# A fused retention and gated-sine MLP kernel: another order of steps for blocks 0 to 2, more casts on GpSimd, and batch 4's keys and values in runs of 64 tokens

## The chip, the core and the metric

The kernel runs on one core of a Trainium2 chip. The core has a tensor engine (PE in the profile), whose weight loads are shown apart (PEld), a vector engine (DVE), a scalar engine (ACT), GpSimd (POOL) and SyncE (SP), which here only issues DMAs. Each engine works through its own list of instructions in order and waits at an instruction until what it needs has been signalled. Sixteen DMA engines move data between HBM and the on-chip memory SBUF; the matmuls write to banks of a second memory, PSUM. The metric is the time of one execution on the device, in microseconds (us).

## The reference

The inputs are q, k and v with 8 batches, 8 heads, 576 tokens and a head size of 64, and the weights of an MLP: `w_in` (512 x 2048), `w_out` (2048 x 512) and `alpha` (2048).

```python
scores = (1 / sqrt(64)) * q @ k.T                 # per batch and head, 576 x 576
ret    = scores * Dmat                            # gamma_h ** (i - j) where i >= j, else 0
attn   = ret @ v                                  # no softmax
x = attn, heads side by side                      # 4608 x 512
h = x @ w_in                                      # 4608 x 2048
g = h + sin(alpha * h) ** 2 / (alpha + 1e-9)
out = g @ w_out                                   # 4608 x 512
```

All inputs and the output are 32-bit floats; on the chip the matmuls take 16-bit operands. Since the decay is a power of the distance between tokens, the kernel puts it into k and q as row factors and carries what lies behind a chunk of 128 tokens in a running state of k times v.

## The kernel before, in words

**Units of work.** The 4608 tokens are cut into nine blocks. Block n (0 to 7) holds the first 512 tokens of batch n; block 8 holds the last 64 tokens of all batches. For each block there are 16 projections (`project(n, fc)`, four matmuls of 128x512 each, L549), each followed by a sine on ACT (`sine`, L557), a square on ACT, VectorE or GpSimd (`square`, L566 or L568) and a product on VectorE (`product`, L573), which gives one sixteenth of g. The second gemm is cut into 16 steps too (`gemm2(n, u)`, L592, four matmuls of 128x512): u = 4c + part adds a quarter of the sum for the c-th 128 rows. After four parts `finish(n, c)` copies the rows out of PSUM and issues two output DMAs (L585).

**Attention of a batch.** It is done in two parts p of 256 tokens. `load(b, nm, p)` brings 512 KB of q, k or v (L148, or L143 for the form in runs of 64 tokens). `cast` turns them to 16 bits with the decay factors (L194 on DVE or POOL; values are copied, L119 or L121). q and k are then transposed: by TensorE (`turn`, L227) with a copy out of PSUM (`take`) in batches 0 and 1, by a DMA transpose on SyncE's queue (`crossed`, L217) from batch 2 on. `outer` makes k times v (L308), which `evict`, `take_sum`, `next_sum` (L337), `more` (L353, L354) and `to_state` (L344, L346) turn into running states. `scores` (L372) gives two heads' worth of products, `masked` (L384) applies the causal mask on VectorE, `values` (L414) and `add_states` (L436) give the attention's output in PSUM, and `keep` copies it to SBUF as x, the left operand of the projections.

**Token order.** Up to batch 4, partition i of a part holds tokens 2i and 2i+1, so one contiguous run of a load is 512 bytes long. From batch `HALVED` = 5 on, k and v are loaded with 64 neighbouring tokens on 64 partitions: a run is 256 bytes long and a load takes four DMAs of 128 KB, but half of the products of every second score group lie above the diagonal and are left out (64 of 128 columns), and so are a quarter of the masked columns.

**Order of the work.** For blocks 0 to 2 the order is a hand-placed list of calls under `tc.manual_schedule()`: the order of calls is the order on each engine, and the PSUM bank of each step is its last argument (h0, h1, h2, op, m0, m1). The table `BUFFERS` says which of the SBUF buffers each load, cast and so on takes in turn. From block 3 to block 8 a loop sets the order: projection u, its sine, attention of the next batch at some u, square, product, second gemm u of the block before. The list ends with batches 0 to 3 done and batch 4 loaded, cast and with its outer products made.

**DMA queues.** All loads of q, k, v, the DMA transposes and the outputs are issued by SyncE, in order; an issue waits until its buffer is free or its data are there, and all issues behind it wait too. `w_in` and `w_out` are loaded by GpSimd in four parts each (L109, L112), which turn them to 16 bits; w_out's rows lie so that each partition reads runs of 8 KB, in this kernel and in the changed one. `wait_for_w_out(g)` (L613) is a small DMA on SyncE that reads a loaded part of w_out, so SyncE stands until that part has landed. `fill_up` does the same `PAD` = 7 times in block 7.

**Fillers.** `keep_busy` (L605) lets TensorE multiply zeros while it has nothing to do at the start.

The changed functions and their callers, with the line numbers of the profile:

## Time and profile before

| | |
|---|---|
| median of 3 runs | 311.7 us (311.09 to 312.0) |
| the profiled execution | 309.53 us, of which its span 307.8 us |
| busy share of the span | PE 95%, DVE 64%, ACT 63%, POOL 42% |
| HBM | 36.75 MB read, 9.44 MB written, 150 GB/s over the span |

The page of the profile gives shares and the costliest groups: a group's line has the source line, engine, operation, the tiles written and read, the shape, the count, the busy time, the mean of one in ns, and the idle time before it with what ended it. A row of the timeline has start, duration, engine, line, operation and tiles. "x12" means twelve instructions merged into a row. A row of SPq is the time in which SyncE's sequencer issued a DMA, not the transfer itself. In the chain of waits a DMA's time runs from its issue to its landing. Matmul ends are modelled, so the distance between starts tells more than the duration of one.

### The profile page before, as it was taken

The numbers are of one execution on the slowest core, as the hardware profiler recorded it, in microseconds if no ns is written. First come the engines' busy times: TensorE is split into PE (matmuls) and PEld (weight loads), VectorE is DVE, ScalarE is ACT, GpSimd is POOL, SyncE is SP. The second block draws the span as 40 slices with busy tenths as digits, with TensorE's granted clock in tenths as the row PEclk, the third lists the DMA queues.
The fourth block names the chain that finished last, engine by engine and source line by source line (L and its number), as shares of the span: only waits on it lengthen the run. The fifth ranks groups of instructions, "written<-read, shape, count | busy, mean of one in ns | idle before, by whom it ended". The sixth has DMA issues, their size and how long they took to land.

```text
span 307.8 us, 7895 instructions
## 1 busy us (share of the span) xinstructions
PE 291.3 (95%) x3225; PEld 156.3 (51%) x3225; DVE 197.2 (64%) x281; ACT 193.3 (63%) x323; POOL 128.9 (42%) x149
## 2 busy tenths in 40 slices
PE   3879999999799999999999999799999999999995
PEld 1758555555355654554455445444455454444443
DVE  2867796968576876867665686556656746655600
ACT  3748877994278668665776577556774456555411
POOL 2767774467664556686159626833030000000000
PEclk9999999999999999999999999999999999999999
DMA  8999999999567398889799969966361121111132
GB/s 222 347 224 213 275 276 324 276 235 238 126 171 207 85 182 190 234 183 150 169 255 169 205 151 269 157 142 144 75 134 38 38 43 39 34 34 34 44 90 74
DMA packets 115620, 49.98 MB, mean 162 GB/s; under 512 B 71424, under 2 KB 110592, under 8 KB 115584
## 3 DMA queue, kind: packets, MB, share of 16 engines
q1 hardware_dynamic: 112064, 45.10, 63.1%
q0 software_dynamic: 2688, 4.19, 7.6%
q8 instruction: 25, 0.41, 0.6%
q10 hardware_dynamic: 832, 0.18, 0.4%
q14 instruction: 11, 0.09, 0.1%
HBM read 36.75 MB, written 9.44 MB: 150 GB/s over the span
## 4 chain that ended last, share of the span: by engine, by line
PE 82%; DMA 7%; issue 3%; POOL 2%; ACT 2%; DVE 2%; SPq 1%; POOLq 0%; DVEq 0%; ACTq 0%
PE ops L592 38%; PE hps L549 36%; PE o L414 2%; PE sc L372 2%; DMA raw<-in_k_dram 2%; DMA raw<-in_q_dram 2%; DMA raw<-in_v_dram 2%; PE kv L308 1%; ACT s L557 1%; DMA qT<-q 1%; POOL w_in L109 1%; SPq L148 1%; PE o L436 1%; DVE ret L384 1%; POOL k L194 1%
## 5 line engine op out<-in xcount | busy, mean ns | idle before, releaser
L592 PE MATMUL ops<-w_out,gT 128*128 128x512 f16 (+2 forms) x592 | 142.6, 374 | 0.1
L557 ACT ACTIVATE s<-hps,alpha_t 128x512 f16<-128x512 f32 x144 | 97.7, 685 | 69.4 <-PE hps L549 67.9
L573 DVE SCALAR_TENSOR_TENSOR gT<-ss,inva,hps 128x512 f16<-128x512 f16 x144 | 105.6, 745 | 52.5 <-ACT ss L566 47.9
L549 PE MATMUL hps<-xT,w_in 128*128 128x512 f16 (+1 forms) x544 | 126.9, 367 | 2.1 <-issue 2.0
L549 PEld LDWEIGHTS <-w_in 128*128 128x128 f16 x608 | 68.0, 114 | 58.2 <-issue 2.2
L592 PEld LDWEIGHTS <-gT 128*128 128x128 f16 x592 | 56.2, 98 | 63.0 <-issue 0.7
L568 DVE TENSOR_TENSOR ss<-s 128x512 f16<-128x512 f16 x62 | 34.9, 562 | 20.6 <-ACT s L557 20.0
L566 ACT ACTIVATE ss<-s 128x512 f16<-128x512 f16 x73 | 46.0, 631 | 1.4
L194 POOL TENSOR_TENSOR k<-raw,cn 128x1024 f16<-128x1024 f32 (+1 forms) x17 | 26.7, 1576 | 34.0 <-DMA raw<-in_k_dram 30.0
L119 ACT COPY osb<-ops 128x512 f32<-128x512 f32 (+1 forms) x33 | 19.2, 581 | 15.2 <-PE ops L592 13.8
L384 DVE TENSOR_TENSOR ret<-sc,mask 128x1024 f16<-128x1024 f32 x20 | 23.8, 1218 | 7.1 <-PE sc L372 7.1
L194 POOL TENSOR_TENSOR q<-raw,cn 128x1024 f16<-128x1024 f32 (+1 forms) x10 | 18.5, 1868 | 2.1 <-DMA raw<-in_q_dram 1.3
L353 POOL TENSOR_TENSOR s<-kvs,cn 128x256 f32<-128x256 f32 x21 | 13.7, 651 | 11.4 <-ACT kvs L119 11.3
L354 POOL TENSOR_TENSOR kvs<-s,kvs 128x256 f32<-128x256 f32 x21 | 16.0, 762 | 3.6 <-ACT kvs L119 2.2
L119 ACT CAST xT<-o 128x1024 f16<-128x1024 f32 (+1 forms) x13 | 12.6, 983 | 7.4 <-PE o L436 7.3
L121 POOL CAST v<-raw 128x1024 f16<-128x1024 f32 (+1 forms) x11 | 11.0, 998 | 14.6 <-DMA raw<-in_v_dram 14.6
L549 PE MATMUL hps<-xS,w_in 128*128 128x512 f16 x64 | 16.4, 379 | 0.0
L178 POOL TENSOR_TENSOR ks<-ks,cn 128x512 f16<-128x512 f32 x4 | 4.2, 1044 | 22.2 <-DMA vs<-in_v_dram 13.6
L568 POOL TENSOR_TENSOR ss<-s 128x512 f16<-128x512 f16 x9 | 9.3, 1038 | 8.9 <-ACT s L557 8.9
L414 PE MATMUL o<-ret,v 64*64 64x128 f16 (+1 forms) x512 | 11.6, 215 | 1.2 <-issue 0.7
L372 PE MATMUL sc<-qT,kT 64*64 64x128 f16 (+1 forms) x512 | 10.7, 215 | 1.8 <-DVE ret L384 1.0
L372 PEld LDWEIGHTS <-kT 64*64 64x64 f16 x512 | 7.6, 107 | 8.5 <-issue 6.7
(57 smaller groups left out, 153.7 us busy)
## 6 DMA issues: line engine op xcount, KB each, us to landing
out_dram<-osb SPq DMA_DIRECT2D x70, 128.0 KB, 2.5
raw<-in_q_dram SPq DMA_DIRECT2D x16, 512.0 KB, 5.9
raw<-in_k_dram SPq DMA_DIRECT2D x10, 512.0 KB
raw<-in_v_dram SPq DMA_DIRECT2D x10, 512.0 KB, 5.7
raw<-in_v_dram SPq DMA_DIRECT2D x24, 128.0 KB, 3.3
raw<-in_k_dram SPq DMA_DIRECT2D x24, 128.0 KB, 3.4
w_in<-in_moe_w_in_dram POOLq DMA_DIRECT2D x4, 512.0 KB, 11.3
w_out<-in_moe_w_out_dram POOLq DMA_DIRECT2D x4, 512.0 KB, 11.5
```

The lines of the kernel that those rows point to most:

```text
L119: eng.copy(d_, s_)
L194: eng.tensor_tensor(dst[:, a0:a1].rearrange("p a r t d -> p t (a r) d"), t_.rearrange("p (t a) x -> p t a x", t=2)[:, :, a0:a1].rearrange( ...
L354: nc.gpsimd.tensor_tensor(self.kvs[:, c], s32, self.kvs[:, c], ADD)
L372: matmul(sc[halves(g), t, c : c + n], kT[halves(t), 2 * a + r, halves(g)], qT[halves(t), 2 * a : 2 * a + 2, 64 * g + i0 : 64 * g + 64], st ...
L384: nc.vector.tensor_tensor(ret.rearrange("p t (z x) -> p (t z) x", z=2)[:, :, 0:n], sc.rearrange("p t (z x) -> p (t z) x", z=2)[:, :, 0:n], ...
L414: made.append(matmul(o[t][halves(e), c : c + 128].rearrange("p (r i) -> p r i", r=2)[:, :, i0:64], v16[halves(g), 4 * t + 2 * x + e, r, :] ...
L549: matmul(hps_of[n, fc][0][:, cols], w_in16[fc // 4][:, a, fc % 4 :: 4], xs[n][:, a, cols], start=(a == 0 and part != 1), stop=(a == KT - 1 ...
L557: nc.scalar.activation(s_t, hps, mybir.ActivationFunctionType.Sin, bias=0.0, scale=alpha_t[:, fc : fc + 1],)
L566: nc.scalar.activation(ss_t, s_t, mybir.ActivationFunctionType.Square)
L568: eng.tensor_tensor(ss_t, s_t, s_t, MULT)
L573: nc.vector.scalar_tensor_tensor(gT[n][:, fc, :], ss_t, inva[:, fc : fc + 1], hps, MULT, ADD)
L592: matmul(ops[n, c, cols.start][:, cols], gT[n][:, fk, c * P : (c + 1) * P], w_out16[:, fk, cols], start=(fk == 0), stop=(fk == FC - 1), sk ...
```

## The change

Four things are changed.

1. The list of steps for blocks 0 to 2 is another one, with another use of PSUM banks and SBUF buffers. q of batch 0 is loaded before v; the fillers have other sizes and places; the fourth part of w_in is loaded behind the third part of w_out; SyncE's first gate watches the fourth part of w_in instead of the first of w_out (the new function `wait_for_w_in`), and there are three more such gates.
2. Casts and squares move between engines. GpSimd casts half of the first k, both parts of batch 1's q, most of batch 2, and all keys and queries of batches 3 and 4; ACT takes values of batches 3 and 4; fewer squares of block 0 are on GpSimd, more on ACT.
3. `HALVED` goes from 5 to 4: k and v of batch 4 too are loaded in runs of 64 tokens, so its scores and masks are the shorter ones. The mask for that form is still made in the loop of block 3.
4. `PAD` goes from 7 to 8, and the loop's cycle of banks starts with h0.

The core of the diff (moved steps are cut where they only change places):

```diff
-    HALVED = 5
+    HALVED = 4
+    def wait_for_w_in(g):
+        nc.sync.dma_start(gate, w_in16[g][:, 0, 0:64])
-    PAD = 7
+    PAD = 8
...
-        keep_busy(3, "op")
+        keep_busy(7, "op", 128)
+        keep_busy(6, "h0", 256)
+        keep_busy(11, "op", 128)
         load(0, "k", 0)
-        load(0, "v", 0)
         load(0, "q", 0)
-        cast(0, "v", 0, A_)
-        invert_alpha()
-        cast(0, "k", 0, V)
+        load(0, "v", 0)
+        cast(0, "k", 0, V, (0,))
+        cast(0, "k", 0, G_, (1,))
         turn(0, "k", 0, "op")
+        cast(0, "q", 0, V, (1,))
+        cast(0, "q", 0, V, (0,))
+        turn(0, "q", 0, "h0")
...
+        load_w_in(1)
+        load_w_in(2)
+        cast(1, "q", 1, G_)
+        at[0].to_state(1, G_)
+        load_w_out(2)
+        cast(1, "q", 0, G_)
+        load_w_in(3)
+        turn(1, "q", 0, "op")
+        at[0].keep(1, V, A_)
+        take(1, "q", 0, V)
+        project(0, 2, "h2", 0)
...
+        load_w_out(3)
+        wait_for_w_in(3)
...
+        load(1, "v", 0)
+        cast(1, "v", 0, G_)
+        gemm2(0, 12, "h2")
+        gemm2(0, 13, "h2")
...
+        load(2, "q", 1)
+        load(2, "k", 1)
+        cast(2, "k", 1, G_)
+        cast(2, "q", 1, V)
+        load(2, "q", 0)
+        cast(2, "q", 0, G_)
+        load(2, "k", 0)
+        load(3, "k", 1)
+        cast(3, "k", 1, G_)
+        load(2, "v", 0)
+        load(3, "k", 0)
+        wait_for_w_out(1)
+        load(2, "v", 1)
+        cast(2, "v", 1, G_)
+        crossed(2, 1, "k")
+        cast(2, "v", 0, G_)
+        cast(2, "k", 0, V)
+        crossed(2, 1, "q")
+        crossed(2, 0, "k")
+        load(4, "q", 1)
+        crossed(2, 0, "q")
+        load(3, "v", 0)
+        load(3, "v", 1)
+        load(4, "v", 0)
+        load(3, "q", 1)
...
+        cast(3, "v", 0, A_, (0,))
+        cast(3, "v", 0, V, (1,))
+        cast(3, "v", 1, A_)
+        at[2].values(1, True)
+        at[2].add_states(1)
+        at[3].outer((0, 1), "op", "h2")
+        at[3].more(1)
+        load(4, "k", 0)
+        load(3, "q", 0)
+        crossed(3, 1, "k")
+        cast(4, "q", 1, G_)
+        cast(3, "q", 1, G_)
+        at[3].more(2)
+        cast(4, "k", 0, G_, (0,))
+        wait_for_w_in(3)
+        load(4, "q", 0)
+        crossed(3, 1, "q")
+        crossed(3, 0, "k")
+        load(4, "k", 1)
+        cast(4, "v", 1, G_)
+        cast(4, "k", 0, G_, (1,))
+        cast(3, "q", 0, G_)
+        cast(4, "q", 0, G_)
+        at[3].more(3)
+        at[3].to_state(3, G_)
+        cast(4, "v", 0, A_)
...
+        cast(4, "k", 1, G_)
+        at[4].outer((0, 1), "op", "h0")
...
+        wait_for_w_out(3)
...
-        h, m = cycle(("h2", "h0", "h1")), cycle(("m0", "m1"))
+        h, m = cycle(("h0", "h1", "h2")), cycle(("m0", "m1"))
```

The removed list for the same steps put GpSimd's casts of batches 3 and 4 between squares and sums one by one, transposed batch 2 by q, k, k, q of parts 0, 0, 1, 1, and loaded k of batch 4 before its q and v.

## The prediction

> **What bounds the kernel.** I read the page first (engine shares and the costliest groups), then busy time by stretches, then TensorE's waits and the timeline around them.

> ```profile
> span 307.8 us, 7895 instructions
> PE 291.3 (95%) x3225; PEld 156.3 (51%) x3225; DVE 197.2 (64%) x281; ACT 193.3 (63%) x323; POOL 128.9 (42%) x149
> L557 ACT ACTIVATE s<-hps,alpha_t 128x512 f16<-128x512 f32 x144 | 97.7, 685 | 69.4 <-PE hps L549 67.9
> L566 ACT ACTIVATE ss<-s 128x512 f16<-128x512 f16 x73 | 46.0, 631 | 1.4
> ```
> ```profile
> 21.26:35.00 13.74, 13.74 (x97) 10.21 (x97) 11.32 (x20) 12.01 (x19) 8.69 (x9) 1.00 1.14 216
> 45.00:75.00 30.00, 29.91 (x338) 15.35 (x336) 23.77 (x33) 24.26 (x46) 17.31 (x17) 1.00 1.07 271
> 75.00:85.00 10.00, 7.79 (x211) 4.51 (x210) 5.71 (x8) 2.30 (x3) 5.71 (x5) 1.00 0.90 151
> 85.00:107.00 22.00, 21.90 (x275) 11.98 (x271) 16.42 (x23) 16.98 (x31) 12.40 (x17) 1.00 0.58 156
> ```

> In the second view the columns are length, then busy PE, weight loads, DVE, ACT, POOL, granted clock, DMA share. TensorE has no idle time worth the name from 21.26 us, the first projection, except 2.21 us in 75 to 85 and the 2.0 us of the next view, which lies in the loop. So the time is the start, plus TensorE's own work, plus holes. The granted clock is 1.00 in each row. The new list can win only at the start and in the first hole; it can lose anywhere up to the loop of blocks 3 to 8, whose order stays. The two holes:

> ```profile
> PE hps L549 <- issue: 2.0, 1, 2.0
> PE o L436 <- issue: 1.3, 1, 1.3
> PE sc L372 <- DMA qT<-q: 0.8, 1, 0.8
> 71.61 5.93 DMA raw<-in_q_dram
> 77.54 3.33 DMA qT<-q
> ```

> The 2.0 is the hole in the loop and the 1.3 half of the first one. "Issue" means that nothing in the trace released them; both follow dense runs of 64x64 matmuls (a guess at a cause: instructions arriving late). The 0.8 has a cause: q of batch 3 loaded at 71.61, its DMA transpose issued at 77.54, 3.33 us to landing, and the scores behind it.

> **The change, part by part.** First the start; these rows carry it.

> ```profile
> 6.55 1.04 ACT L119 CAST v<-raw 128x1024 f16<-128x1024 f32 x1 [3.20 <-DMA raw<-in_v_dram]
> 9.46 0.85 DVE L337 SCALAR_TENSOR_TENSOR kvs<-kvs,cn,kv 128x64 f32<-128x64 f32 x4
> 9.68 2.04 POOL L194 TENSOR_TENSOR k<-raw,cn 128x512 f16<-128x512 f32 x2 [6.66 <-DMA raw<-in_k_dram]
> 11.05 1.75 DVE L194 TENSOR_TENSOR q<-raw,cn 128x1024 f16<-128x1024 f32 x1 [0.74 <-DMA raw<-in_q_dram]
> 11.66 3.53 POOL L109 DMA_DIRECT2D w_in<-in_moe_w_in_dram  x4
> 12.70 1.03 ACT L119 COPY kT<-tr 128x1024 f16<-128x1024 f16 x1
> 13.95 4.62 DVE L384 TENSOR_TENSOR ret<-sc,mask 128x1024 f16<-128x1024 f32 x4 [0.54 <-PE sc L372]
> 15.19 1.93 POOL L194 TENSOR_TENSOR q<-raw,cn 128x1024 f16<-128x1024 f32 x1
> 19.18 0.61 POOL L346 TENSOR_TENSOR s<-kvs,cn 128x256 f16<-128x256 f32 x1
> 19.73 0.60 POOL L112 DMA_DIRECT2D w_out<-in_moe_w_out_dram  x1
> 20.71 0.40 PE L436 MATMUL o<-qT,s 64*64 64x128 f16 x16
> 47.37 0.42 DVE L346 TENSOR_TENSOR sS<-kvs,cn 128x256 f16<-128x256 f32 x1 [0.62 <-POOL kvs L354]
> 21.18 0.69 DVE L121 CAST xT<-o 128x512 f16<-128x512 f32 x1 [2.61 <-PE o L436]
> 21.26 1.98 PE L549 MATMUL hps<-xT,w_in 128*128 128x256 f16 x12 [0.15 <-ACT xT L119]
> 23.08 0.61 PE L227 MATMUL tr<-ident,q 128*128 128x128 f16 x8
> ```

> Loads arrive 1.5 us apart (second 6.55, fourth 9.68, fifth 11.05). The new order loads q before v and splits k's cast, so by the fifth load (q, second part) both transposes of the first part are done and the first scores stand at about 12.0: v's cast 8.05 to 9.1 on ACT, two copies of about 1.03 to 11.15, scores. VectorE then runs from 11.05 without a gap: cast 1.75, four masks 4.62, two running sums 1.70, one state 0.42, half of the first keep 0.69, ending at 20.2. GpSimd goes 11.72, three weight issues 2.65, cast of q 1.93, state 0.61, w_out issue 0.60, the second q's cast 1.93: 19.4. TensorE adds the state matmuls (0.40) and the transpose of batch 1's q (0.61) after 19.6: the first projection starts at 20.7, with that transpose behind it, where before it stood in front at 23.08. Gain 21.26 + 0.61 - 20.7 = 1.2 us. VectorE's chain could also give 0.5 more (that cast at 1.2 instead of 1.75) or, if the scores come at 13.5, nothing: ends 0 and 1.7, taken 1.2. The fillers on TensorE (41 before, 36 now) stand where it waits for these engines and are free; if one runs late it delays a transpose by its own length, which the lower end takes in.

> Block 0. Sixteen projections each need a sine (0.685) and a square; ACT's squares go from 6 to 9 (+1.9 us), but two copies of transposed q and k (2.0) leave it: even. VectorE takes these copies and loses a cast of q to GpSimd: even. GpSimd: three squares fewer, two casts of q and k as rows above. The weights' gate on SyncE now watches the fourth w_in transfer instead of the first w_out; both are the fifth transfer of that queue, so I take the same instant for it and the value load behind it, which before went out at 31.60:

> ```profile
> 31.60 5.85 DMA raw<-in_v_dram
> 55.07 1.04 POOL L121 CAST v<-raw 128x1024 f16<-128x1024 f32 x1
> 109.01 1.03 PE L549 MATMUL hps<-xT,w_in 128*128 128x512 f16 x4
> 109.88 1.03 PE L592 MATMUL ops<-w_out,gT 128*128 128x512 f16 x4
> ```

> A projection or second-gemm unit is 0.865 (the last two starts). Counting from 20.7, TensorE reaches batch 1's outer products at 38.7; v lands at 37.45 and GpSimd needs 1.04 for the whole cast: 38.5. No hole, 0.2 to spare. The last w_out transfer is now issued ahead of loads that it used to follow (34.7 by GpSimd's walk); those loads are used 5 us later or more, so the swap costs nothing, or at most the 0.2 if it gets ahead of v too and then some 2 us more.

> Blocks 1 and 2. From the first projection to the loop both kernels do 48 projections and 32 second gemms. The new list, with 0.865 a unit, 0.6 a transpose, 0.42 for lone scores and 0.3 for the second of a pair, 0.45 for a single and 0.65 to 0.7 for a double outer product, and about 2.0 for one batch's values with their states:

> 20.7 to 49.8: 27 units (23.4), two transposes (1.2), four scores (1.7), two single outer products (0.9), values (2.0).
> 49.8 to 73.4: 23 units (19.9), batch 2's outer products, scores (1.5) and values.
> 73.4 to 105.2: 30 units (25.9), two double outer products (1.4), batch 3's scores (1.6) and values (2.2), and two holes: 0.35 at batch 3's outer products (half of v cast on VectorE behind a mask), 0.3 at the bank behind them.

> At 49.8 block 1's projections start, where before it was 49.75 with one second gemm less done. I set ACT, VectorE and GpSimd beside this walk with their group means and looked at each reuse of a PSUM bank: in block 1 ACT does 22 us of work in 23.6 and VectorE as much, so margins are 0.2 to 1 us, but none is broken except the two. Before, the loop's first projection starts at 107.1: it is the 25th to 28th of the run of 28 below, less the pipeline's tail (102.80 + 5 x 0.865). The loop thus starts 1.9 us earlier, the 1.2 included.

> ```profile
> 36.03 1.40 SPq L148 DMA_DIRECT2D raw<-in_k_dram  x1
> 102.80 5.52 PE L549 MATMUL hps<-xT,w_in 128*128 128x512 f16 x28
> 110.05 5.35 SPq L143 DMA_DIRECT2D raw<-in_k_dram  x8
> 122.73 0.64 PE L372 MATMUL sc<-qT,kT 64*64 64x128 f16 x32
> 153.72 0.54 PE L372 MATMUL sc<-qT,kT 64*64 64x128 f16 x32
> L354 POOL TENSOR_TENSOR kvs<-s,kvs 128x256 f32<-128x256 f32 x21 | 16.0, 762 | 3.6 <-ACT kvs L119 2.2
> L353 POOL TENSOR_TENSOR s<-kvs,cn 128x256 f32<-128x256 f32 x21 | 13.7, 651 | 11.4 <-ACT kvs L119 11.3
> ```

> Batch 4 in runs of 64 tokens: its two score pairs save 0.10 each in the loop (0.64 against 0.54): 0.2 us; its masks get shorter on VectorE, which has room. Its k and v take 2.7 us of queue per 512 KB (eight issues, 5.35) against 1.40: four such loads, +5.1 us on SyncE and the DMA between 60 and 90 us. They stand in front of the transposes of batch 3. My queue count puts the last transpose that the scores at 88.6 need at 84: it waits for GpSimd's cast of q (80.7), then 3.33. Cover 4 us, so nothing is paid. If that cover is gone the whole 5.1 can fall on TensorE; ends 0 and 5.1, taken 0, because the DMA share was 0.58 in 85 to 107. [...]

> GpSimd from 75.7 to 93.8 is one unbroken queue: five whole casts of 1.9, one v cast 1.04, two half casts 1.0 (2.04 for the pair), three sums of 0.65 + 0.76, two states 0.61; batch 4's outer products need its end at 95.8. Cover 2.0.

> The mask of the halved form, five short instructions on GpSimd in the loop's second unit, is now needed in its fourth; that queue reaches its end near 109.8, the need is at 111.5: free.

> Sum: -1.9 (of it 1.2 start, 0.7 holes) - 0.2 + 0.1 for waits of the "issue" kind, which I leave where they are though they may move (1.3 and 2.0 seen; between -2 and +2): -2.0. The profiled execution took 309.53 with its span of 307.8, so 307.5; the median shown is 311.7, 2.2 above it, and the same difference gives 309.7.

> **Rivals.** (a) The start gains and the hole stays: the transposes of batch 3 arrive as late as before. For it: the same in-order SyncE queue. Against it: q of batch 3's second part is loaded before the outputs now. Gain 1.2 + 0.2, less 0.65 for the two new holes: 311.0, within 0.3% (the 0.9 us about which this kernel can be told from no change).

> (b) Slower: SyncE's queue decides. Sixteen small issues of batch 4 add 5.1 us, and with outputs waiting for ACT in the same queue the transposes of batch 3's q miss 88.6. It ends slower once they land 7 us later than my 84. If the cover of 4 is eaten by other waits and all 5.1 shows: 309.7 + 5.1 = 314.8. Against it: half the DMA was free after 85.

> ```profile
> 93.96 1.23 DVE L194 TENSOR_TENSOR q<-raw,cn 128x1024 f16<-128x1024 f32 x1 [2.57 <-issue]
> ```

> (c) GpSimd decides: casts stretch. The 11.05 cast took 1.75 on VectorE beside a GpSimd cast, where its group elsewhere takes 1.23; the same ratio on the 12.5 us of casts in 75.7 to 93.8 is +5.3, less 2.0 cover: +3.3, 313.0. Against it: that GpSimd cast itself took 2.04 for its two halves and another 1.93, with VectorE busy beside both. [...]

> **Chances.** Forecast 0.62 (its own range 308.7 to 310.7, down to 307.7 if "issue" holes vanish); (a) 0.13, (b) 0.16, (c) 0.09. So faster by over 0.3% 0.62, within it 0.13, slower 0.25. The range runs from 307.7 to 313.5: past (c) and into (b), not to its end.

> **What would show it.** First projection near 20.7; VectorE unbroken from the fifth load; no wait of the scores for a DMA near 80 to 90; GpSimd's queue done by 94; the loop's first projection near 105; scores in the loop's first block at 0.54. It is wrong if the scores of batch 2 or 3 wait for a transpose, if outer products wait for casts, or if new "issue" holes appear beside the longer dense run of batch 2's values and batch 3's outer products.

## The result and the profile after

The changed kernel takes 308.61 us (306.0 to 309.51, 6 runs) against 311.69 (309.82 to 312.12, 6 runs) beside it: a ratio of 0.990, 95% interval 0.985 to 0.995. Another 12 runs, later, gave 0.991 (0.987 to 0.995). Runs more than 1.5% above the fastest of their kernel count as slow; the ratios, and the medians of the experiments below, leave them out. The profiled execution is one of its slowest, 309.48 with a span of 307.5; so this one trace is only 0.3 us shorter than that of before, and the gain has to be looked for with more traces than one.

Busy time of the changed kernel by stretches (columns as in the prediction), then TensorE's waits by cause:

```profile
45.00:75.00 30.00, 27.54 (x353) 14.40 (x352) 21.75 (x30) 20.54 (x35) 19.99 (x20) 0.94 1.01 256
75.00:85.00 10.00, 9.90 (x189) 5.37 (x188) 6.12 (x10) 6.77 (x13) 3.66 (x4) 1.00 0.77 187
85.00:107.00 22.00, 21.91 (x303) 11.71 (x301) 14.90 (x19) 16.94 (x33) 17.93 (x19) 1.00 0.80 166
67.00:70.00 3.00, 3.00 (x22) 1.29 (x23) 1.88 (x2) 0.50 (x1) 2.76 (x5) 0.50 0.93 235
190.00:200.00 10.00, 10.00 (x190) 5.59 (x189) 6.13 (x8) 7.79 (x13) 6.42 (x9) 1.00 0.84 181
```
```profile
PE sc L372 <- DMA qT<-q: 2.4, 1, 2.4
PE tr L227 <- POOL k L194: 1.9, 2, 1.7
...
PE hps L549 <- DMA w_in<-in_moe_w_in_dram: 0.7, 1, 0.7
```

The hole of 75 to 85 is closed (9.90 of 10 us busy, 7.79 before), and the stretch of the loop that held the other hole is full. No wait is put down to "issue" any more, where before had 2.0, 1.3 and 0.7. In their place stand waits with a cause, and 3 us in which the granted clock was 0.50. The timeline shows where, after and then before:

```profile
19.73 0.62 PE L227 MATMUL tr<-ident,q 128*128 128x128 f16 x8
21.05 8.93 PE L549 MATMUL hps<-xT,w_in 128*128 128x256 f16 x56 [0.69 <-DMA w_in<-in_moe_w_in_dram]
...
34.37 0.60 POOL L112 DMA_DIRECT2D w_out<-in_moe_w_out_dram  x1
38.85 0.45 PE L308 MATMUL kv<-v,k 64*64 64x64 f16 x32
40.82 1.90 POOL L194 TENSOR_TENSOR k<-raw,cn 128x1024 f16<-128x1024 f32 x1 [1.45 <-DMA raw<-in_k_dram]
42.78 0.62 PE L227 MATMUL tr<-ident,k 128*128 128x128 f16 x8 [1.65 <-POOL k L194]
66.99 0.64 PE L372 MATMUL sc<-qT,kT 64*64 64x128 f16 x16 [2.37 <-DMA qT<-q]
67.56 4.15 PE L549 MATMUL hps<-xT,w_in 128*128 128x512 f16 x12
93.60 0.64 PE L372 MATMUL sc<-qT,kT 64*64 64x128 f16 x32
110.14 1.03 PE L592 MATMUL ops<-w_out,gT 128*128 128x512 f16 x4
```
```profile
19.29 0.75 PE L414 MATMUL o<-ret,v 64*64 64x128 f16 x18 [0.74 <-issue]
78.03 0.30 PE L436 MATMUL o<-qT,s 64*64 64x128 f16 x5 [1.27 <-issue]
108.15 1.03 PE L592 MATMUL ops<-w_out,gT 128*128 128x512 f16 x4
193.74 0.41 PE L436 MATMUL o<-qT,s 64*64 64x128 f16 x16
194.08 0.41 PE L549 MATMUL hps<-xT,w_in 128*128 128x512 f16 x1
196.45 0.81 PE L549 MATMUL hps<-xT,w_in 128*128 128x512 f16 x3 [1.96 <-issue]
```

The rows at 110.14 and 108.15 are the same instructions in both kernels, the loop's first second gemm; below they are called the mark. In this execution the new list reaches the mark 2.0 us later than the old one, and from there to the end it takes 197.4 us (307.5 - 110.14) where before took 199.7. What was to be gained ahead of the loop is lost there, and what was gained came inside the loop, whose order did not change.

### The profile page after: what moved, and what is told of

The parts are those of the page before. It is cut to its first block, busy times and chain, and to the rows that moved or that the text cites. A ratio compares the mean times of both kernels' runs of the same rounds, so it can differ in the third digit from the quotient of the medians.

```text
span 307.5 us, 7881 instructions
## 1 busy us (share of the span) xinstructions
PE 293.8 (96%) x3208; PEld 156.1 (51%) x3208; DVE 190.1 (62%) x280; ACT 193.8 (63%) x322; POOL 136.4 (44%) x151
## 4 chain that ended last, share of the span: by engine, by line
PE 82%; DMA 10%; POOL 3%; SPq 2%; issue 1%; ACT 0%; DVE 0%; DVEq 0%; ACTq 0%; POOLq 0%
PE ops L592 39%; PE hps L549 36%; DMA w_in<-in_moe_w_in_dram 4%; PE o L414 2%; DMA qT<-q 2%; SPq L148 2%; PE sc L372 2%; DMA raw<-in_q_dram 2%; DMA raw<-in_v_dram 2%; POOL q L194 1%; PE kv L308 1%; PE o L436 1%; POOL k L194 1%; POOL v L121 0%; PE os L497 0%
## 5 line engine op out<-in xcount | busy, mean ns | idle before, releaser
L592 PE MATMUL ops<-w_out,gT 128*128 128x512 f16 (+2 forms) x592 | 142.5, 374 | 0.1
L557 ACT ACTIVATE s<-hps,alpha_t 128x512 f16<-128x512 f32 x144 | 97.6, 685 | 70.4 <-PE hps L549 68.3
L549 PE MATMUL hps<-xT,w_in 128*128 128x512 f16 (+1 forms) x532 | 127.5, 375 | 0.7 <-DMA w_in<-in_moe_w_in_dram 0.7
L549 PEld LDWEIGHTS <-w_in 128*128 128x128 f16 x596 | 66.9, 114 | 59.8 <-issue 2.0
L592 PEld LDWEIGHTS <-gT 128*128 128x128 f16 x592 | 56.0, 98 | 62.3 <-issue 0.4
L566 ACT ACTIVATE ss<-s 128x512 f16<-128x512 f16 x73 | 45.9, 631 | 1.4
L568 DVE TENSOR_TENSOR ss<-s 128x512 f16<-128x512 f16 x63 | 33.2, 528 | 20.4 <-ACT s L557 19.8
L194 POOL TENSOR_TENSOR k<-raw,cn 128x1024 f16<-128x1024 f32 (+1 forms) x17 | 30.5, 1795 | 27.1 <-DMA raw<-in_k_dram 27.1
L119 ACT COPY osb<-ops 128x512 f32<-128x512 f32 (+1 forms) x34 | 19.7, 580 | 16.6 <-PE ops L592 15.1
L194 POOL TENSOR_TENSOR q<-raw,cn 128x1024 f16<-128x1024 f32 x13 | 24.5, 1902 | 2.1 <-DMA raw<-in_q_dram 2.0
L384 DVE TENSOR_TENSOR ret<-sc,mask 128x1024 f16<-128x1024 f32 x16 | 19.1, 1218 | 3.7 <-PE sc L372 3.6
L353 POOL TENSOR_TENSOR s<-kvs,cn 128x256 f32<-128x256 f32 x21 | 13.3, 633 | 10.6 <-ACT kvs L119 10.4
L354 POOL TENSOR_TENSOR kvs<-s,kvs 128x256 f32<-128x256 f32 x21 | 15.3, 727 | 4.2 <-ACT kvs L119 1.7
L549 PE MATMUL hps<-xS,w_in 128*128 128x512 f16 x64 | 16.4, 379 | 0.0
L121 POOL CAST v<-raw 128x1024 f16<-128x1024 f32 x10 | 10.3, 1036 | 11.5 <-DMA raw<-in_v_dram 10.6
L384 DVE TENSOR_TENSOR ret<-sc,mask_halved 128x768 f16<-128x768 f32 x16 | 15.2, 949 | 0.0
L178 POOL TENSOR_TENSOR ks<-ks,cn 128x512 f16<-128x512 f32 x4 | 4.2, 1042 | 22.7 <-DMA vs<-in_v_dram 11.4
L119 ACT CAST xT<-o 128x1024 f16<-128x1024 f32 (+1 forms) x15 | 12.9, 878 | 1.7 <-PE o L436 1.6
L372 PE MATMUL sc<-qT,kT 64*64 64x128 f16 (+1 forms) x512 | 10.7, 219 | 2.5 <-DMA qT<-q 2.4
L346 POOL TENSOR_TENSOR s<-kvs,cn 128x256 f16<-128x256 f32 x17 | 10.9, 645 | 4.6 <-ACT kvs L119 3.0
L372 PEld LDWEIGHTS <-kT 64*64 64x64 f16 x512 | 7.8, 111 | 9.7 <-issue 8.4
```

Of the source, the lines that this page charges most:

```text
L119: eng.copy(d_, s_)
L194: eng.tensor_tensor(dst[:, a0:a1].rearrange("p a r t d -> p t (a r) d"), t_.rearrange("p (t a) x -> p t a x", t=2)[:, :, a0:a1].rearrange( ...
L353: nc.gpsimd.tensor_tensor(s32, self.kvs[:, c - 1], g1.unsqueeze(2).to_broadcast([P, 4, D]), MULT)
L354: nc.gpsimd.tensor_tensor(self.kvs[:, c], s32, self.kvs[:, c], ADD)
L372: matmul(sc[halves(g), t, c : c + n], kT[halves(t), 2 * a + r, halves(g)], qT[halves(t), 2 * a : 2 * a + 2, 64 * g + i0 : 64 * g + 64], st ...
L384: nc.vector.tensor_tensor(ret.rearrange("p t (z x) -> p (t z) x", z=2)[:, :, 0:n], sc.rearrange("p t (z x) -> p (t z) x", z=2)[:, :, 0:n], ...
```

## The experiments

**Both kernels again.** No edit. These two further profiles ask which waits belong to a kernel and which to one execution.

> The kernel before, unchanged, for a second profile of it. Theory A (the hole of 2.0 us in the loop at 194 us belongs to the kernel's instruction stream): the hole stands again at the same matmul, within 0.2 us of 2.0, and the 1.3 us hole at 78 us too. Theory B (such holes are chance of one execution): either is gone or stands elsewhere. Span 307 to 309 us.

> The changed kernel, unchanged, for a second profile. The wait of TensorE for the DMA transpose of batch 2's q (2.4 us at 64.6) and for GpSimd's cast of batch 1's k (1.7 us at 41.1) come back within 0.5 us if they belong to the order; the stretch of half clock at 67 to 70 us comes back if the idle time causes it, and is gone or elsewhere if it is chance. No hole in the loop.

They took 310.77 and 306.47 us. Rows of before, and the clock behind its hole; then rows of after:

```profile
195.97 0.81 PE L549 MATMUL hps<-xT,w_in 128*128 128x512 f16 x3 [2.08 <-issue]
197.00:200.00 3.00, 3.00 (x8) 1.04 (x7) 1.45 (x2) 1.40 (x2) 2.76 (x5) 0.51 1.10 83
```
```profile
PE tr L227 <- POOL k L194: 3.3, 2, 2.8
107.57 1.03 PE L592 MATMUL ops<-w_out,gT 128*128 128x512 f16 x4
```

The loop's hole returns at the very same matmul; the one at 78 does not, and one of 0.5 us stands at 46.68 instead. In the changed kernel the wait for GpSimd's cast of k returns (2.8), the one for the transposed q and the half clock at 67 to 70 do not, and the mark stands at 107.57 instead of 110.14. A third profile of the changed kernel, taken later, has both waits (2.63 and 1.46). So the waits ahead of the mark differ from one execution of the changed kernel to the next.

**The length of TensorE's stream alone.** The new list has 17 matmuls fewer ahead of the loop than the old one: 5 fillers, and 12 because it makes fewer projections in halves (40 of 128x256, not 64). Each is a weight load and a matmul (the pages count 3225 of both before, 3208 after), so in the loop TensorE's instructions stand 34 places earlier. Two kernels exchange only this, by their fillers.

```
# before, shifted                       # after, shifted back
-        keep_busy(22, "h2", 128)       -        keep_busy(11, "op", 128)
+        keep_busy(5, "h2", 512)        +        keep_busy(28, "op", 48)
```

> The kernel before with 17 fewer fillers at the start (22 of 128 columns become 5 of 512), so that every later TensorE instruction stands 34 places earlier in its stream, as in the changed kernel; nothing else is touched. If the loop's hole hangs on where the dense run of matmuls falls in the stream: the hole of 2.0 us is gone and the time is 2 us (0.6%) below the kernel before. Rival (the hole hangs on the other engines and DMAs): hole stays, same time within 0.3%.

> The changed kernel with 17 more fillers at the start (11 of 128 columns become 28 of 48), so that its later TensorE instructions stand where those of the kernel before stood. If the place in the stream makes the hole: a hole of about 2 us in the loop near 195 us, and the time 2 us above the changed kernel's, about 310.6. Rival: no hole, 308.6.

The old list with the shift takes 307.12 us, 0.990 of before (0.986 to 0.993): as fast as the changed kernel. The new list shifted back takes 309.7 (12 runs, 306.88 to 312.97), 0.998 (0.993 to 1.002): the gain is gone, and a hole of 2.6 us stands in the loop. Old list shifted, then new list shifted back:

```profile
190.00:200.00 10.00, 10.00 (x190) 5.64 (x189) 4.49 (x8) 7.35 (x12) 7.06 (x10) 1.00 0.98 170
47.80 0.36 PE L436 MATMUL o<-qT,s 64*64 64x128 f16 x11 [1.28 <-issue]
107.14 1.03 PE L592 MATMUL ops<-w_out,gT 128*128 128x512 f16 x4
```
```profile
198.83 0.81 PE L549 MATMUL hps<-xT,w_in 128*128 128x512 f16 x3 [2.61 <-issue]
```

So the shift explains the gain as far as these intervals can tell, and the list itself, with batch 4 in runs of 64, is worth about nothing. The gain does not come from the start: the first projection stands at 21.24 with the shift and at 21.26 before. Nor is it the hole's length alone. Of the 15 runs of before that enter its median beside these, six had a mean granted clock of 0.998 or more, and their median is 309.0 us, 1.9 above the shifted kernel, the length of the hole; the other nine had 0.988 to 0.995, and their median is 311.1. All six runs of the shifted kernel had 0.998 or more. How a hole of 2 us can cost clock as well is shown in the section on the hardware.

**Half the shift, and other fillers.** 16 places from the same spot; then 34 places from two spots.

```
# half                                  # other fillers
-        keep_busy(22, "h2", 128)       -        keep_busy(22, "h2", 128)
+        keep_busy(14, "h2", 192)       +        keep_busy(16, "h2", 176)
                                        -        keep_busy(14, "h1", 64)
                                        +        keep_busy(3, "h1", 298)
```

> The kernel before with 8 fillers fewer, so TensorE's stream stands 16 places earlier instead of 34. Theory, the place in the stream decides whether the loop's hole appears: all or nothing, either the hole of some 2 us at 194 to 199 stays (310.8 to 311.5) or it is gone (307 to 308). Rival, the gain comes from the start (fewer fillers to run) and grows with their number: 309.0 to 309.6, with the loop's hole unchanged and the first projection earlier.

> The kernel before with the same 34 places taken out as in the first shifted run, but 11 of the 17 fillers at another spot of the start. Theory, only the number of instructions ahead of the loop counts: no hole in the loop, 307.1 (306.3 to 308.0). Rival, it was the fillers beside the first sums that cost time there: about 311 with the loop's hole in place.

307.38 us (0.990, 0.985 to 0.995) and 307.82 (0.993, 0.990 to 0.996). Which fillers go makes no difference that these runs can tell, and the first projection starts at 21.13 and 21.05, so the rival of the start falls too. The expectation of all or nothing fails: with 16 places the loop's hole is 0.57 us long and stands eight matmuls further down, behind five of the second gemm:

```profile
193.95 1.24 PE L592 MATMUL ops<-w_out,gT 128*128 128x512 f16 x5
195.76 0.81 PE L592 MATMUL ops<-w_out,gT 128*128 128x512 f16 x3 [0.57 <-issue]
```

That row points to the cause. Counting all of TensorE's instructions in the compiled programs from 0 (in before 3225 weight loads, 3225 matmuls, and 29 semaphores, drains and branches), the first matmul behind this hole is number 4802, and so it is in the three traces with the long hole. All "issue" holes in front of TensorE's matmuls, in all 14 traces of this study, fall into five places:

```
place   194 + 256 k   seen in
450-451   k = 1       before 0.7, again 0.8, shifted 0.7, half 0.5, other 0.2, shifted halved 0.7
1218      k = 4       again 0.5, shifted 1.3, other 1.0, shifted halved 1.0
1987      k = 7       before 1.3
4035      k = 15      other 0.2, changed kernel without halving 0.7
4802      k = 18      before 2.0, again 2.1, half 0.6, new list shifted back 2.6
```

("Again" is the second profile of before; six of the 14, all of the changed kernel or of edits of it, have none.) Seventeen holes, each within one place of 194 + 256 k, whatever instruction stands there. The page's table of DMA queues has the other half of it, the same row before and after (packets, MB, share):

```profile
q8 instruction: 25, 0.41, 0.6%
```

25 packets of 0.41 MB / 25 = 16.4 KB make one packet per 259 of TensorE's 6479 instructions: read so, its program arrives in blocks, and the page counts their 0.6% on the same 16 DMA engines as the 63.1% of q1, most of the data. The times of these packets in the traces tie them to the places. Each of the 17 holes, at place 194 + 256 k, ends 2.2 to 2.6 us after packet number k - 1 (from 0) has started; and at none of these places, 24 in each of the 14 traces, does TensorE go on less than 2.2 us after its packet. A hole, as these times read, is what is left of the 2.2 to 2.6 us when TensorE has run through a block before the next one is there. In before the stretch that ends at 4802 holds 64x64 matmuls and, as its last, one of 128x512; from its start (the 26th matmul of the batch at 192.10, 192.4) to the end of the hole it is 4.05 us, in the repeated run 4.2, in the half shift 4.3, in the new list shifted back 4.65. With 34 places less the stretch takes in 18 matmuls of 0.216 and lasts 5.5 us: no hole. The length of a stretch does not decide alone. In the changed kernel the 256 instructions ahead of place 4035 take 1.6 us and no hole follows; the packet that belongs to that place had started 0.6 us before the first of them.

**Batch 4 in runs of 64, alone.** First on the old list with the shift, where no hole in the loop disturbs; then taken back from the changed kernel.

```
# shifted before                        # after
-    HALVED = 5                         -    HALVED = 4
+    HALVED = 4                         +    HALVED = 5
```

> The kernel before with the 17 fillers taken out as in the shifted run (307.1 us), plus batch 4 in runs of 64 tokens. If the prediction's step on batch 4 is right (0.2 us saved in the scores, transfer time covered): 306.9, no new wait of TensorE for a DMA. Rival, transfers decide: four loads cost 5.1 us more of queue and some of it shows in front of batch 3's scores: 308.5 to 312, with a wait of the scores for the transposed q or of the outer products for raw loads between 75 and 100 us. The loop's hole should stay away, since the instruction stream keeps its length.

> The changed kernel with batch 4 left in runs of 128 tokens as before. If halving is worth its 0.2 us and its transfers are covered: 308.8 against 308.6, with the same waits at 41 to 43 (k's cast) and for the transposed q at 65 to 67. Rival, the longer loads cost something: below 308, and then with a shorter wait for a DMA somewhere in 60 to 95.

On the old list it takes 311.38 us, a ratio of 1.000 (0.997 to 1.003) where the shift alone had 0.990: it costs some 3 us, against the theory and within the rival's 308.5 to 312. Rows of the old list halved, then of the shifted run without it:

```profile
88.51 2.74 SPq L143 DMA_DIRECT2D raw<-in_k_dram  x4
91.29 0.63 SPq L148 DMA_DIRECT2D raw<-in_q_dram  x1
96.61 1.23 DVE L194 TENSOR_TENSOR q<-raw,cn 128x1024 f16<-128x1024 f32 x1 [4.97 <-issue]
98.55 1.02 PE L549 MATMUL hps<-xT,w_in 128*128 128x512 f16 x4 [1.55 <-DVE gT L573]
110.37 1.03 PE L592 MATMUL ops<-w_out,gT 128*128 128x512 f16 x4
```
```profile
87.75 0.41 SPq L148 DMA_DIRECT2D raw<-in_k_dram  x1
88.22 0.64 SPq L148 DMA_DIRECT2D raw<-in_q_dram  x1
93.13 1.23 DVE L194 TENSOR_TENSOR q<-raw,cn 128x1024 f16<-128x1024 f32 x1 [2.51 <-issue]
```

The k load is four issues of 2.74 us in all instead of one of 0.41, so the q load behind it on SyncE goes out 3.1 us later, VectorE stands at its cast 3.5 us later, and TensorE waits for a product (gT) queued behind that cast. The mark moves from 107.14 to 110.37. Of these 3.2 us, 1.55 are that wait; the scores at 81.26 also wait 1.35 us for the transposed q, against 0.16, but traces of the old list without the halving have such waits of up to 1.35 too. In the changed kernel the same halving is not dearer: without it 309.41 us, 0.993 (0.990 to 0.997), against 0.991 with it, no difference that these runs can tell. From mark to end, traces without a loop hole take 198.0 us with batch 4 in runs of 128 (shifted, other fillers) and 197.1 to 197.6 with runs of 64 (after, its second profile, and the old list shifted and halved). So in the new list the halving costs nothing that these runs can tell; which of its moved loads makes the room was not tried. And from the mark on the halving returns 0.4 at most: the shifted trace has a wait of 0.27 in the loop that the halved one lacks, which leaves 0.2.

**The new waits.** Three edits of the changed kernel try to remove what it lost at 41 and 65: the last part of w_out issued behind the v cast; that and batch 2's last q transposes ahead of a load of batch 4; the transposes and a wait of SyncE for that w_out ahead of batch 2's loads.

```
# w_out later                           # and the transposes
-        load_w_out(3)                  -        load(4, "q", 1)
...                                              crossed(2, 0, "q")
         cast(1, "v", 0, G_)            +        load(4, "q", 1)
+        load_w_out(3)
# gate (with the transposes, load_w_out(3) where it was)
+        wait_for_w_out(3)
         load(2, "q", 1)
```

> The changed kernel with the last part of block 0's w_out issued behind GpSimd's cast of batch 1's v, no longer ahead of it. Theory, the early issue puts that transfer ahead of k's load and so makes TensorE wait 1.65 to 2.8 us for k's cast: the wait goes, 306.0 to 306.9. Rival 1, k's load is late for another reason (its buffer, SyncE's queue): the wait stays, 308.6. Rival 2, the second gemm now waits for w_out itself: a wait of TensorE for w_out of 1 to 2 us, 308 to 309.

> As the run before, and on SyncE the transposes of batch 2's second q part issued ahead of the load of batch 4's second q part. Theory, that load delays the transposes on which the scores at 64 to 67 wait (0 to 2.4 us): 0.5 to 1.5 us below the run with w_out alone, 305.0 to 306.2, no wait of the scores for the transposed q above 0.5. Rival, the delay comes from the value load issued at 51.4 and the cast behind it: no difference from the run with w_out alone.

> The changed kernel unchanged, beside the other runs of this call: 308.6, ratio 0.99; no hole in the loop, waits for k's cast near 41 in every profile, for the transposed q only in some.

> The changed kernel with SyncE waiting for the last part of block 0's w_out before it issues batch 2's loads, and the transposes of batch 2's second q part ahead of batch 4's q load. Theory, at 35 to 46 the transfers themselves are the bound and batch 2's loads take the share of k and w_out: k's wait (1.65 to 2.8) falls to 0.5 or less and none for w_out takes its place, 306 to 307. Rival, the loads held back are then late in turn: the wait moves to batch 2's casts or transposes at 50 to 67, 308 to 310.

309.51 us (0.994, 0.990 to 0.997), 309.64 (0.995, 0.992 to 0.998) and 308.95 (0.994, 0.991 to 0.997); the changed kernel beside the last of them 308.0 (0.991, 0.987 to 0.995). None gains. With w_out later, and then with the gate:

```profile
42.35 0.62 PE L227 MATMUL tr<-ident,k 128*128 128x128 f16 x8 [0.77 <-POOL k L194]
46.78 1.02 PE L592 MATMUL ops<-w_out,gT 128*128 128x512 f16 x4 [2.37 <-DMA w_out<-in_moe_w_out_dram]
```
```profile
42.52 0.48 SPq L617 DMA_DIRECT2D gate<-w_out  x1
42.41 1.90 POOL L194 TENSOR_TENSOR k<-raw,cn 128x1024 f16<-128x1024 f32 x1 [2.39 <-DMA raw<-in_k_dram]
44.36 0.62 PE L227 MATMUL tr<-ident,k 128*128 128x128 f16 x8 [2.59 <-POOL k L194]
92.54 0.64 PE L372 MATMUL sc<-qT,kT 64*64 64x128 f16 x32 [1.31 <-DMA qT<-q]
```

The first rival of the later issue falls and the second holds: k comes sooner, and the second gemm waits for w_out instead, 2.37 us. So w_out, issued ahead of v, does delay k, but both are needed before 47 us, and whichever goes first makes the other late. The gate's theory falls: with batch 2's loads held back until 42.5, k is as late as ever (2.59), and batch 3's transposes are now late too (1.31). Batch 2's loads were not what k waited behind. The wait for batch 2's transposed q is absent from both traces with the edit of the transposes, but also from three traces of kernels without that edit, and the time did not move; so the edit is not shown to remove it.

## Why the prediction came out right, and where it was wrong

309.7 was forecast for the median and 308.6 measured, inside the range, and "faster" was right. The mechanism was mostly not the one the sum names, so the number came out by luck: 1.9 of its 2.0 us were to come from an earlier start of the loop, and what was measured comes from the holes that the sum left in place.

- **Holes of the "issue" kind, +0.1 in the sum, "left where they are".** This is the term that failed. They came to 4.0 us before and to nothing after. The shift alone takes away the 2.0 in the loop, leaves 2.0 ahead of it, and moves the median by 3.1 us beside its own runs of before (307.12 against 310.17). The guess at their cause, instructions arriving late, is what the 17 places and the packets' 2.2 to 2.6 us point to, and the places could have been counted: the stream's length follows from the two lists, and the instruction queue's row stood on the page.
- **The loop starts 1.9 us earlier.** It does not. The mark stands at 110.14, 107.57 and 111.78 in the three traces of the changed kernel, against 108.15 and 107.45 in the old one: new waits for k's cast and for batch 2's transposed q take what the walk had gained.
- **The start, 1.2 us.** VectorE's chain and the transpose came as walked (first projection ready at 20.36, the transpose done before it at 19.73), but w_in's first part landed 0.69 later: 0.8 gained. And 0.74 of the old start was itself a hole of the "issue" kind, at place 451.
- **Block 0's last w_out "costs nothing, or at most the 0.2 ... and then some 2 us more".** The outer products came at 38.85 for 38.7, but k, not v, paid: 1.65 and 2.8 us at its transpose. "Used 5 us later or more" was no cover: k landed at 40.82, its cast takes 1.90, and TensorE was ready for its transpose at 41.13.
- **Batch 2's transposes.** The walk names no cover for them; they cost 0, 1.46 and 2.37 in the three traces. For batch 3 the step was right: no wait at 93.60.
- **Halving.** Scores at 0.54 in the loop and transfers covered, as said. The gain is 0.2 to 0.4 for the 0.2 of the sum. But the 2.7 and 1.40 us that the prediction sets against each other, for the DMA as well as for SyncE, are rows of SPq, the time of issuing: single issues of a k load take 0.40 to 3.62 us in the trace of before, so the 5.1 is no measure of transfer. Rival (b) describes what the halving does on the old list, 3.2 us at the mark, though half of it through VectorE's queue and not through the transposes.
- **GpSimd's queue and the mask** had the room they were given: no wait of batch 4's products.

## What to carry to other kernels

The waits here that nothing released, 17 of 0.2 to 2.6 us, all stood within one place of 194 + 256 k and ended 2.2 to 2.6 us after an instruction packet had started. So at such a wait, count all instructions of the engine from the start, and see whether the holes keep to fixed places. Before a reordering is credited with 1%, make a kernel that only shifts the stream by the same number of instructions; here 17 fillers fewer in the old list gave all that these runs can tell. And a transfer moved can make the next one late: with w_out issued behind v, the wait for k came to 0.77 us, where three profiles without that edit had 1.65 to 2.8, and one of 2.37 for w_out took its place.

## What was not expected of the hardware

```profile
193.64:197.06 3.42, 1.34 (x7) 0.53 (x6) 0.11 (x1) 1.63 (x3) 3.19 (x6) 1.00 1.17 172
197.06:200.47 3.41, 3.41 (x10) 1.21 (x9) 1.45 (x2) 1.34 (x2) 3.10 (x6) 0.50 1.12 108
```
```profile
39.40:42.82 3.42, 2.02 (x31) 0.77 (x18) 2.10 (x3) 0.37 (x1) 0.84 (x2) 1.00 1.08 299
42.82:46.23 3.41, 2.03 (x45) 1.28 (x46) 0.91 (x3) 1.04 (x1) 3.25 (x5) 1.00 1.02 289
46.23:49.64 3.41, 3.41 (x68) 1.58 (x68) 3.41 (x3) 1.41 (x5) 2.60 (x4) 1.00 1.10 331
```

So 2.08 us of idle time inside one stretch went with half the clock in the next, and 2.78 spread over two did not. In before the hole of 1.96 is cut too, by a border at 195.76: the two stretches hold 1.27 and 0.69.

Left open: what decides when an instruction packet is asked for (they start between 4.6 us before and 4.8 us after the first instruction of a block), how long one takes when the DMA engines are idle (their share was 0.8 or more at every hole in the loop), and why the changed kernel's transposes of batch 2 are late in some executions only.
